# A fused linear attention and ELU feed-forward: the second group's attention by rows and DMA transposes

## The chip, the core and the metric

The kernel runs on one core of one Trainium2 chip. The metric is the device time of one execution in microseconds (us). A core has five engines, each with an instruction queue of its own that it works through in order: TensorE (PE in the profile, with PEld for its weight loads), VectorE (DVE), ScalarE (ACT), GpSimd (POOL) and SyncE (SP, which here only issues DMAs). Matmul results are written to PSUM, everything else lives in SBUF. Sixteen DMA engines move data between memory and SBUF, and can transpose on the way.

## The reference

Eight batches, eight heads, 576 positions, head size 64; then a feed-forward layer with 512 inputs, 2048 hidden units and 512 outputs for all 4608 tokens. Cut to its core:

```python
kv  = np.einsum('bhsd,bhse->bhde', k, v)          # one 64x64 matrix per batch and head
out = np.einsum('bhsd,bhde->bhse', q, kv)
rms = np.sqrt(np.mean(out * out, axis=-1, keepdims=True) + 1e-06)
x   = (out / rms * g_norm)                        # then laid out as 4608 x 512
h   = x @ w_in
g   = np.where(h > 0.0, h, np.exp(np.minimum(h, 0.0)) - 1.0)
result = g @ w_out
```

All matmuls take bf16 inputs and sum in fp32.

## The kernel before, in words

The tokens are worked in nine groups (0 to 8, called `T`) of 512. A position inside a batch is split into 9 slots of 64 rows, so a group holds eight slots, of one or two batches (`slot_of`, line 75).

For each group three things are done: the attention, which gives `xT` (the normed attention output, features on the partitions); the first product, eight tiles `mm1(T, i)` of eight 128x512 matmuls each (line 378), whose results `h_ps` go through the ELU into `gT`; and the second product into `o_ps` (line 399), 64 matmuls, called here in eight halves of eight matmuls: `mm2_half(T, n)` is row block `n // 2` and, by `n % 2`, the first or last half of the 16 hidden blocks. The finished row block is copied by ACT (line 415) and stored by SP.

The ELU of a tile has an ACT part, the exponential of `h_ps` (line 350), and a DVE part, `rest()`: `min(e, 1) - 1` (line 358) and then a maximum with `h_ps` (line 362). DVE thus reads `h_ps` last, and the PSUM buffer of the tile is free when the rest is done. With `relu=True` ACT also writes `relu(h_ps)` (line 354), the buffer is free after that, and DVE adds two SBUF tiles instead.

Attention comes in two forms.

- By columns (`Turned`, line 216): q is transposed by matmuls against an identity (`q_t_mm`, line 174) and copied into `qT`; the product with `kv` gives the output already turned (`y_mm`, line 189); ACT squares it; a matmul with a block of ones sums the squares (`mean_mm`, line 199); ACT takes the inverse root (lines 208, 209); DVE scales into `xT` (line 212).
- By rows (`attention`, line 258): q is loaded raw in fp32 (`fetch_ahead`), cast and reordered by POOL (`cast_q`, line 103) and turned by two DMA transposes issued by SP (`turn_q`, line 331). Per half of the group (`h` 0 and 1) the pieces are: `se`, 16 or 24 small matmuls (line 250) into the one buffer named `at` and ACT's square of it; `sum`, DVE's sums (line 283); `inv`, two small ACT steps (lines 291, 292); `mul`, DVE's scaling out of `at` (line 299) and two DMA transposes on SP into `xT` (line 306); `gain`, DVE's factor `g` on `xT` (line 312). The piece `kv` is the k-v product, also into `at`.

`after_turn` puts a tiny POOL copy (the gate, line 339) that waits for the turned q; the next loads stand behind it on POOL.

The order is written out by hand: the framework keeps each engine's instructions in program order and adds the waits. Before the change, group 0 and 1 have attention by columns, and group 2 too: its pieces (`late_kv`, `late_q`, `late_y`, `late_norm`, lines 697 to 717) stand between the tiles of group 1's first product and then between four halves of group 1's second product (lines 728 to 741). From group 3 on attention is by rows, inside `window` (line 747): tiles of the first product of group `T`, pieces of attention of `T + 1` and halves of the second product of `T - 1` alternate.

The kernel's PSUM pools hold eight buffers of 128x512 fp32. The tags A and B are a pair of them each, m two single ones, x two single ones in use until `start_psum.close()`, after which the same space is the `at` buffer, of which there is one. A matmul into a buffer waits until the last reader of its former content is done.

Apart from the first few, all loads are issued by POOL in the order of lines 484 to 508, each waiting for the load eight before it.

Of the kernel before, what the change touches and what calls it, by code (L numbers as in the profile page):

```python
# [16 lines left out]
def kernel(  # L17
# [14 lines left out]
    P = 128  # L32
# [48 lines left out]
    def fetch(name, b, u=None):  # L81

        if (name, b) not in bf:
            bf[name, b] = qkvp.tile([P, 4, RK, D], BF16, name=f"{name}_bf", tag=name)
        ms = slice(0, 4) if u is None else slice(u, 4, 2)
        load(bf[name, b][:, ms], name, b, ms)
# [5 lines left out]
    def fetch_ahead(b):  # L92
        raw[b] = stage.tile([P, 4, RK, D], FP32, name="st_q", tag="q")
        load(raw[b], "q", b)
        for name in "kv":
            fetch(name, b)
# [32 lines left out]
    def single(tag, name):  # L129
        pool = ps_x if tag == "x" else ps_m2  # L130
        return pool.tile([P, 512], FP32, name=name, tag=tag)

    def pair(tag, name):
        if tag in "xm":
            return [single(tag, name) for _ in range(2)]
        return ps_m1.tile([P, 2, 512], FP32, name=name, tag=tag)

    def as_bf16(ps):
        return ps.bitcast(BF16)
# [3 lines left out]
    def qT_tile(b):  # L143
        qT[b] = attp.tile([P, 2, 2, RK, 64], BF16, name="qT", tag="qT", bufs=3)
        return qT[b]

    def x_tile(T):
        xT[T] = attp.tile([P, KC, G], BF16, name="xT", tag="xT")
        return xT[T]

    def kv_mm(b, kv_ps, u, ls=range(2)):
        for j in range(RK):
            for s in range(2):
                rows = slice(s * 64, s * 64 + 64)
                for l in ls:
                    nc.tensor.matmul(  # L156
                        kv_ps[s][l * 64 : l * 64 + 64, u * 64 : u * 64 + 64],
                        lhsT=bf["k", b][rows, 2 * l + u, j, :],
                        rhs=bf["v", b][rows, 2 * l + u, j, :],
                        start=(j == 0),  # L160
                        stop=(j == RK - 1),
                    )

    def kv_out(b, kv_ps, u, engs):
        for s in range(2):
            copy_on(engs[s], kv_sb[:, b, u, s], kv_ps[s][:, u * 64 : u * 64 + 64])
# [4 lines left out]
    def q_t_mm(b, u, js, dst):  # L171
        for n, j in enumerate(js):
            for l in range(2):
                nc.tensor.transpose(  # L174
                    dst[l * 64 : l * 64 + 64, n * P : n * P + P], bf["q", b][:, 2 * l + u, j, :], ident
                )

    def q_t_out(b, u, eng, src, js):
        copy_on(eng, qT[b][:, :, u, js, :], src.rearrange("p (j s r) -> p s j r", s=2, r=64))
# [148 lines left out]
    def turn_q(b):  # L328
        qt = qT_tile(b)
        for s in range(2):  # L330
            nc.sync.dma_start_transpose(
                out=qt[:, s].rearrange("p u j r -> p (u j) r"),
                in_=bf["q", b][s * 64 : s * 64 + 64].rearrange("p u j l d -> p (u j l d)"),
            )

    def after_turn(b):

        gate = const.tile([1, 2, 16], BF16, name="gate")
        nc.gpsimd.tensor_copy(out=gate, in_=qT[b][0:1, :, 1, RK - 1, 0:16])  # L339
# [46 lines left out]
    def mm1(T, i, tag, relu=False):  # L386
        if i == 0:
            g_tile(T)
        ps = pair(tag, "h_ps")
        mm1_part(T, i, ps, range(KC))  # L390
        return elu(T, i, ps, relu)

    o_ps, o_sb = {}, {}
# [53 lines left out]
    def mm2_half(T, i):  # L447
        mm2(T, i // 2, 8 * (i % 2), 8 * (i % 2) + 8)
# [52 lines left out]
    for name in "kvq":  # L501
        fetch(name, 1, 1)
    load_w_out(3)
    for u in range(2):
        for name in "qkv":
            fetch(name, 2, u)
    fetch_ahead(3)
    cast_q(3)

# [11 lines left out]
    def turned_q(b, u, tag):  # L521

        ps = as_bf16(single(tag, "qt_ps"))
        q_t_mm(b, u, range(8), ps)
        return ps
# [42 lines left out]
                stop=(c == KC - 1),  # L568
            )

    qT_tile(0)
    x_tile(0)
    g_tile(0)
    g_ps = pair("A", "g_ps")
# [72 lines left out]
    def mm2_all(f0, f1, js=(2, 3, 0, 1)):  # L647
        for f in range(f0, f1):
            for j in js:
                mm2(0, j, f, f + 1)  # L650
# [4 lines left out]
            o_ps[0, j0 + t] = ps[:, t, :]  # L655

    x_tile(1)
    qT_tile(1)
    for u in range(2):
        n = Turned(1, u)  # L660
        if u == 0:
            mm2_all(0, 4, (2, 3))
        kv_ps = [single("x", "kv_ps") for _ in range(2)]
        kv_mm(1, kv_ps, u)
        kv_out(1, kv_ps, u, (A, A))
        if u == 0:
            mm2_all(0, 4, (0, 1))
        main = turned_q(1, u, "m")
        q_t_out(1, u, V, main, slice(0, 8))
        ends = as_bf16(single("m", "qt_ps"))  # L670
        for t in range(2):
            q_t_mm(t, u, (8,), ends[:, t * P : t * P + P])
        for t in range(2):
            q_t_out(t, u, V, ends[:, t * P : t * P + P], slice(8, 9))
        mm2_all(*((4, 6), (10, 11))[u])
        n.product([single("x", "y_ps") for _ in range(2)])
        for l in range(2):
            n.square(l)
        mm2_all(*((6, 7), (11, 12))[u])
        for l in range(2):  # L680
            n.sums(l, single("m", "mean"))
            n.inv(l)
            n.scale(l)
        mm2_all(*((7, 10), (12, 15))[u])
    for js in ((2, 3), (0, 1)):
        for j in js:
            mm2(0, j, 15, 16, out=False)
        for j in js:
            mm2_out(0, j)

    qT_tile(2)
    x_tile(2)
    n2 = [Turned(2, 0), Turned(2, 1)]

    def late_kv(u, tag):
        kv_ps = pair(tag, "kv_ps")
        kv_mm(2, kv_ps, u)
        kv_out(2, kv_ps, u, (A, A))  # L700

    def late_q(u, tag):
        main = turned_q(2, u, tag)
        end = as_bf16(single(tag, "qt_ps"))
        q_t_mm(2, u, (8,), end[:, 0:P])
        q_t_out(2, u, A, main, slice(0, 8))
        q_t_out(2, u, V, end[:, 0:P], slice(8, 9))

    def late_y(u):
        n2[u].product(pair("xm"[u], "y_ps"))  # L710
        for l in range(2):
            n2[u].square(l)

    def late_norm(u, l):
        n2[u].sums(l, single("mx"[u], "mean"))
        n2[u].inv(l)
        n2[u].scale(l)

    pieces = {
        1: lambda: late_kv(0, "x"),  # L720
        2: lambda: late_kv(1, "m"),
        3: lambda: late_q(0, "x"),
        4: lambda: (late_q(1, "m"), turn_q(3), after_turn(3), fetch_ahead(4)),
        5: lambda: late_y(0),
        6: lambda: late_norm(0, 0),
        7: lambda: late_norm(0, 1),
    }
    for i, tag in enumerate("mBABABAB"):
        rest = mm1(1, i, tag)
        rest()  # L730
        if i in pieces:
            pieces[i]()
    for j, tag in enumerate("AB"):
        o_ps[1, j] = pair(tag, "o_ps")[:, 0, :]
    mm2_half(1, 0)
    late_y(1)
    mm2_half(1, 2)
    late_norm(1, 0)
    mm2_half(1, 1)
    late_norm(1, 1)  # L740
    mm2_half(1, 3)
    start_psum.close()
    ps_at = ctx.enter_context(tc.tile_pool(name="ps_at", bufs=1, space=bass.MemoryType.PSUM))

    def window(T, at, early, late, second):
        for i in range(8):
            rest = mm1(T, i, "AB"[i % 2])
            for name in early.get(i, ()):  # L750
                at[name]()
            if i in second:
                second[i]()
            rest()
            for name in late.get(i, ()):
                at[name]()

    for T in range(2, NT):
        at, early, late = {}, {}, {}
        if T + 1 < NT:  # L760
            at = attention(T + 1)
            if T + 2 < B:
                cast_q(T + 2)

                def ahead(b=T + 2):
                    turn_q(b)
                    if b + 1 < B:
                        after_turn(b)
                        fetch_ahead(b + 1)
                at["ahead"] = ahead  # L770
            else:
                at["ahead"] = lambda: None
            early = {2: ("sum0", "inv0"), 4: ("sum1", "inv1"), 5: ("gain0",), 7: ("gain1",)}
            late = {0: ("kv",), 1: ("se0",), 2: ("mul0",), 3: ("se1",), 4: ("mul1", "ahead")}
        if T == 2:
            early = {2: ("sum0", "inv0"), 5: ("sum1", "inv1"), 6: ("gain0",), 7: ("gain1",)}
            late = {0: ("kv",), 1: ("se0",), 2: ("mul0",), 4: ("se1",), 5: ("mul1", "ahead")}
        halves = {0: 4, 2: 5, 4: 6, 6: 7} if T == 2 else {0: 1, 1: 3, 2: 4, 3: 5, 4: 6, 5: 7}
        second = {i: (lambda n=n: mm2_half(T - 1, n)) for i, n in halves.items()}
        window(T, at, early, late, second)  # L780
        mm2_half(T, 0)
        mm2_half(T, 2)
# [33 lines left out]
```

## Time and profile before

| | |
|---|---|
| median of 9 runs | 292.03 us (291.77 to 292.22) |
| the profiled execution | 292.11 us |
| its span, first to last instruction | 290.3 us |
| mean granted TensorE clock | 0.998 |
| PE busy | 279.9 us, 2109 matmuls seen |
| DVE busy | 165.8 us |
| ACT busy | 141.8 us |
| first matmul of the first product of group 1 | 48.69 us |
| of group 2 | 75.43 us |
| of group 3 | 101.97 us |

The last three are taken from the trace in order of time and the chain of waits. A line of the profile names the source line, engine, operation, output and input tiles, shape and count; behind the bar stand the group's busy time, the mean of one in ns, and the idle time of the engine ahead of it with what ended that. In a line in order of time, the bracket holds the same. Some matmul records are missing from a trace.

### The profile page before, as it was taken

To read this page: it belongs to the slowest core of one execution; us is meant where nothing else is said; L and a number is where in the kernel's file an instruction comes from. 1 tells how busy PE (TensorE), PEld (TensorE's weight loads), DVE (VectorE), ACT (ScalarE), POOL (GpSimd) and SP (SyncE) were. 2 spreads that over 40 slices of the span, in tenths; PEclk is the share of its full clock that TensorE was granted. 3 is DMA by queue.
4 is the path that set the end of the run, shared out by engine and by line. 5 is a ranking of instruction groups with operands and counts; after the bars stand their busy time and mean duration, and the time that the engine had idled before them with its cause. 6 is when DMAs were issued, how large, how long until landed. Compare 5 with 4: busy or idle time off the path is not lost.

```text
span 290.3 us, 5146 instructions
## 1 busy us (share of the span) xinstructions
PE 279.9 (96%) x2109; PEld 130.2 (45%) x2145; DVE 165.8 (57%) x223; ACT 141.8 (49%) x207; POOL 47.1 (16%) x85
## 2 busy tenths in 40 slices
PE   8899999999999999999999999999999999999994
PEld 3444444443444444444444444444444444444443
DVE  2349632776368747863776377636774776344600
ACT  3578358587555435543554255525552555343320
POOL 7643341404200022203400330000000000000000
PEclk9999999999999999999999999999999999999999
DMA  7999999997901299958965894452340215020222
GB/s 212 183 204 206 207 206 236 305 193 207 194 2 36 46 170 240 172 99 231 217 81 92 220 238 79 86 107 72 38 102 6 75 36 108 0 75 0 72 75 73
DMA packets 46332, 37.77 MB, mean 130 GB/s; under 512 B 26468, under 2 KB 40036, under 8 KB 46308
## 3 DMA queue, kind: packets, MB, share of 16 engines
q0 software_dynamic: 15312, 20.71, 36.8%
q1 hardware_dynamic: 30592, 16.19, 27.2%
q10 hardware_dynamic: 404, 0.53, 0.5%
q8 instruction: 17, 0.28, 0.4%
q14 instruction: 7, 0.06, 0.1%
HBM read 36.70 MB, written 9.44 MB: 159 GB/s over the span
## 4 chain that ended last, share of the span: by engine, by line
PE 88%; DVE 4%; ACT 3%; DMA 2%; issue 1%; SPq 0%; DVEq 0%
PE o_ps L399 40%; PE h_ps L378 39%; DMA first_v<-in_v_dram 2%; PE h_ps L563 2%; DVE gT L362 2%; PE at L250 2%; PE at L156 1%; ACT elu_e L350 1%; PE kv_ps L156 1%; PE qt_ps L174 1%; DVE xT L212 1%; PE mean L199 1%; PE y_ps L189 1%; DVE elu_e L358 1%; ACT rT L209 1%
## 5 line engine op out<-in xcount | busy, mean ns | idle before, releaser
L399 PE MATMUL o_ps<-w_out_sb,gT 128*128 128x512 bf16 x548 | 129.2, 379 | 1.3 <-DVE gT L362 0.6
L378 PE MATMUL h_ps<-xT,w_in_sb 128*128 128x512 bf16 x530 | 126.9, 379 | 1.9 <-DVE gT L362 0.6
L350 ACT ACTIVATE elu_e<-h_ps 128x1024 bf16<-128x1024 f32 (+1 forms) x77 | 73.8, 974 | 91.6 <-PE h_ps L378 79.7
L362 DVE TENSOR_TENSOR gT<-elu_e,h_ps 128x1024 bf16<-128x1024 bf16 (+1 forms) x74 | 84.6, 1148 | 7.2
L399 PEld LDWEIGHTS <-gT 128*128 128x128 bf16 x560 | 54.3, 98 | 66.5 <-issue 2.0
L378 PEld LDWEIGHTS <-w_in_sb 128*128 128x128 bf16 x552 | 52.4, 98 | 62.4 <-issue 1.7
L358 DVE TENSOR_SCALAR elu_e<-elu_e 128x1024 bf16<-128x1024 bf16 x72 | 31.6, 440 | 69.4 <-ACT elu_e L350 69.2
L415 ACT COPY o_sb<-o_ps 128x512 f32<-128x512 f32 x32 | 18.4, 587 | 18.9 <-PE o_ps L399 18.1
L103 POOL CAST q_bf<-st_q 128x384 bf16<-128x384 f32 x30 | 14.4, 523 | 28.0 <-DMA st_q<-in_q_dram 24.3
L212 DVE SCALAR_TENSOR_TENSOR xT<-y_ps,g_col,rT 128x512 bf16<-128x512 f32 (+1 forms) x14 | 9.1, 671 | 15.4 <-ACT rT L209 13.4
L283 DVE TENSOR_REDUCE ss<-sq 128x16 f32<-128x1024 bf16 x12 | 14.6, 1219 | 4.6 <-ACT sq L277 4.5
L299 DVE TENSOR_TENSOR xs<-at,ss 128x1024 bf16<-128x1024 f32 x12 | 14.6, 1216 | 0.0
L277 ACT ACTIVATE sq<-at 128x1024 bf16<-128x1024 f32 x12 | 12.3, 1028 | 1.0 <-PE at L250 1.0
L339 POOL COPY gate<-qT 1x32 bf16<-1x32 bf16 x4 | 0.8, 200 | 72.0 <-DMA qT<-q_bf 72.0
L156 PEld LDWEIGHTS <-k_bf 64*64 64x64 bf16 x576 | 6.5, 107 | 6.4 <-issue 6.4
L90 POOL DMA_DIRECT2D k_bf<-in_k_dram x12 | 8.4, 700 | 5.4 <-DMA w_out_sb<-in_moe_w_out_dram 2.1
L90 POOL DMA_DIRECT2D v_bf<-in_v_dram x12 | 8.3, 693 | 5.7 <-DMA w_in_sb<-in_moe_w_in_dram 2.1
L208 ACT ACTIVATE rT<-mean,eps_col 128x512 f32<-128x512 f32 (+1 forms) x9 | 6.6, 730 | 2.4 <-PE mean L199 2.2
L229 ACT ACTIVATE sq<-y_ps 128x512 bf16<-128x512 f32 x8 | 4.3, 596 | 6.5 <-PE y_ps L189 6.5
L112 DVE COPY o_sb<-o_ps 128x256 f32<-128x256 f32 x1 | 0.4, 423 | 11.5 <-DMA out_dram<-o_sb 11.5
L312 DVE TENSOR_SCALAR xT<-xT,g_col 128x1024 bf16<-128x1024 bf16 x12 | 5.7, 478 | 1.7 <-DMA xT<-xs 1.7
L519 PE MATMUL kv_ps<-zeros 128*128 128x512 bf16 x13 | 5.3, 574 | 1.2 <-DVE one L512 1.2
(56 smaller groups left out, 110.5 us busy)
## 6 DMA issues: line engine op xcount, KB each, us to landing
out_dram<-o_sb SPq DMA_DIRECT2D x24, 256.0 KB, 3.9
st_q<-in_q_dram POOLq DMA_DIRECT2D x5, 1152.0 KB, 7.6
k_bf<-in_k_dram POOLq DMA_DIRECT2D x5, 576.0 KB, 10.9
v_bf<-in_v_dram POOLq DMA_DIRECT2D x5, 576.0 KB, 13.6
out_dram<-o_sb SPq DMA_DIRECT2D x19, 128.0 KB, 2.6
w_out_sb<-in_moe_w_out_dram POOLq DMA_DIRECT2D x4, 512.0 KB, 15.0
q_bf<-in_q_dram POOLq DMA_DIRECT2D x5, 288.0 KB, 13.4
k_bf<-in_k_dram POOLq DMA_DIRECT2D x4, 288.0 KB, 14.2
```

The source lines that it names most:

```text
L90: eng.dma_start(out=dst.rearrange("p m j d -> p m (j d)"), in_=in_[:, ms, :])
L103: nc.gpsimd.tensor_copy(out=bf["q", b][:, u, js], in_=raw[b][:, u::2, js, :].rearrange("p l j d -> p j l d"),)
L156: nc.tensor.matmul(kv_ps[s][l * 64 : l * 64 + 64, u * 64 : u * 64 + 64], lhsT=bf["k", b][rows, 2 * l + u, j, :], rhs=bf["v", b][rows, 2 * ...
L277: nc.scalar.activation(sq, st["se", h], AF.Square)
L283: nc.vector.reduce_sum(out=ss, in_=st.pop(("sq", h)).rearrange("p l (m e) -> p (l m) e", e=D), axis=AX.X,)
L299: nc.vector.tensor_tensor(out=st["xs"][:, 2 * h : 2 * h + 2, :].rearrange("p i (l m e) -> p l i m e", l=2, e=D), in0=se_ps.rearrange("p l ...
L350: nc.scalar.activation(e[:, lo:hi, :], h, AF.Exp)
L358: nc.vector.tensor_scalar(out=e, in0=e, scalar1=1.0, scalar2=1.0, op0=ALU.min, op1=ALU.subtract)
L362: nc.vector.tensor_tensor(out=gT[T][:, 2 * i + lo : 2 * i + hi, :], in0=e[:, lo:hi, :], in1=h, op=ALU.add if relu else ALU.max,)
L378: nc.tensor.matmul((ps[a] if isinstance(ps, list) else ps[:, a, :])[:, cols], lhsT=w_in_sb[:, c, f * P : f * P + P], rhs=xT[T][:, c, cols] ...
L399: nc.tensor.matmul(o_ps[T, j], lhsT=gT[T][:, f, j * P : j * P + P], rhs=w_out_sb[:, f, :], start=(f == 0), stop=(f == FC - 1),)
L415: nc.scalar.copy(o_sb[T, half][:, j % 2, :], o_ps[T, j])
```

## The change

Group 2's attention goes from columns to rows. Its q, k and v are loaded whole (q raw), cast by POOL, and q is turned by DMA ahead of batch 3's loads. Its kv product stands behind tile 2 of group 1's first product, its first row product behind tile 3, its second behind tile 6. Tiles 4, 5 and 7 of group 1 take the relu form of the ELU, the tiles' PSUM tags become m, B, A, m, B, A, m, B, and DVE's sums and scalings of group 2 stand ahead of the rests of tiles 4 to 7. Five halves of group 1's second product follow (row blocks 0 and 1 whole, and the first half of block 2), then the two gains; the last three halves stand in group 2's window, where there were four. The tags of every window's tiles swap from A, B to B, A. The transposes of group 2 and the turn of batch 3 on SP now stand after group 1's tiles. In group 0's second product, which stands between the steps of group 1's attention, the stretch behind the first half's scaling grows from hidden blocks 7 to 9 to blocks 7 to 10, and the one behind the second half's shrinks by one block.

```diff
@@ loads
-    for u in range(2):
-        for name in "qkv":
-            fetch(name, 2, u)
+    for b in range(2):
+        qT_tile(b)
+    fetch_ahead(2)
+    cast_q(2)
+    turn_q(2)
+    after_turn(2)
     fetch_ahead(3)
     cast_q(3)
@@ group 0's second product, group 1's attention
-        mm2_all(*((4, 6), (10, 11))[u])
+        mm2_all(*((4, 6), (11, 12))[u])
...
-        mm2_all(*((6, 7), (11, 12))[u])
+        mm2_all(*((6, 7), (12, 13))[u])
...
-        mm2_all(*((7, 10), (12, 15))[u])
+        mm2_all(*((7, 11), (13, 15))[u])
@@ group 1's first product and group 2's attention
-    pieces = {
-        1: lambda: late_kv(0, "x"),
-        2: lambda: late_kv(1, "m"),
-        3: lambda: late_q(0, "x"),
-        4: lambda: (late_q(1, "m"), turn_q(3), after_turn(3), fetch_ahead(4)),
-        5: lambda: late_y(0),
-        6: lambda: late_norm(0, 0),
-        7: lambda: late_norm(0, 1),
-    }
-    for i, tag in enumerate("mBABABAB"):
-        rest = mm1(1, i, tag)
-        rest()
-        if i in pieces:
-            pieces[i]()
-    for j, tag in enumerate("AB"):
-        o_ps[1, j] = pair(tag, "o_ps")[:, 0, :]
-    mm2_half(1, 0)
-    late_y(1)
-    mm2_half(1, 2)
-    late_norm(1, 0)
-    mm2_half(1, 1)
-    late_norm(1, 1)
-    mm2_half(1, 3)
     start_psum.close()
     ps_at = ctx.enter_context(tc.tile_pool(name="ps_at", bufs=1, space=bass.MemoryType.PSUM))
+    at = attention(2)
+    rest = {}
+    for i, tag in enumerate("mBAmBAmB"):
+        rest[i] = mm1(1, i, tag, i in (4, 5, 7))
+        if i == 2:
+            at["kv"]()
+        if i == 3:
+            at["se0"]()
+        if i == 5:
+            at["sum0"]()
+            at["inv0"]()
+            at["mul0"]()
+            rest[4]()
+        if i == 6:
+            at["se1"]()
+            rest[5]()
+        if i < 4:
+            rest[i]()
+    at["sum1"]()
+    at["inv1"]()
+    rest[6]()
+    at["mul1"]()
+    rest[7]()
+    turn_q(3)
+    after_turn(3)
+    fetch_ahead(4)
+    ps = pair("A", "o_ps")
+    for j in range(2):
+        o_ps[1, j] = ps[:, j, :]
+    for f0, f1 in ((0, 8), (8, 12)):
+        for j in range(2):
+            mm2(1, j, f0, f1)
+    mm2_half(1, 4)
+    for j in range(2):
+        mm2(1, j, 12, 16, out=False)
+    for j in range(2):
+        mm2_out(1, j)
+    at["gain0"]()
+    at["gain1"]()
@@ windows
-            rest = mm1(T, i, "AB"[i % 2])
+            rest = mm1(T, i, "BA"[i % 2])
...
-        halves = {0: 4, 2: 5, 4: 6, 6: 7} if T == 2 else {0: 1, 1: 3, 2: 4, 3: 5, 4: 6, 5: 7}
+        halves = {1: 5, 3: 6, 5: 7} if T == 2 else {0: 1, 1: 3, 2: 4, 3: 5, 4: 6, 5: 7}
```

More of the change, by code (lines that the diff above doesn't have):

```diff
@@ L569, in early @@
             )
-    qT_tile(0)
     x_tile(0)
@@ L657 @@
     x_tile(1)
-    qT_tile(1)
     for u in range(2):
@@ L689 @@
             mm2_out(0, j)
[L693 to L717, printed above, removed]
-    pieces = {
-        1: lambda: late_kv(0, "x"),
-        2: lambda: late_kv(1, "m"),
-        3: lambda: late_q(0, "x"),
-        4: lambda: (late_q(1, "m"), turn_q(3), after_turn(3), fetch_ahead(4)),
-        5: lambda: late_y(0),
-        6: lambda: late_norm(0, 0),
-        7: lambda: late_norm(0, 1),
-    }
-    for i, tag in enumerate("mBABABAB"):
-        rest = mm1(1, i, tag)
-        rest()
-        if i in pieces:
-            pieces[i]()
```

## The prediction

> **What bounds the kernel now.** I read the page's busy shares first, then its slices, then stretches of time around the change, then the queues of the loads, then instruction groups. All times below are microseconds (us) from the start of the profiled execution.
>
> The page, busy time and slices:
> ```profile
> PE 279.9 (96%) x2109; PEld 130.2 (45%) x2145; DVE 165.8 (57%) x223; ACT 141.8 (49%) x207; POOL 47.1 (16%) x85
> ...
> DVE  2349632776368747863776377636774776344600
> ...
> PEclk9999999999999999999999999999999999999999
> DMA  7999999997901299958965894452340215020222
> ```
> TensorE (PE) is busy nearly always at full clock, so a gain must come from fewer matmuls or from PE's few idle stretches; and the DMA engines are full until slice 9 (65 us). Stretches of time (length, then busy time per engine):
> ```profile
> 50.00:60.00 10.00, 9.55 (x141) 4.83 (x141) 6.75 (x10) 6.33 (x13) 2.94 (x6) 1.00 1.11 303
> 60.00:70.00 10.00, 8.91 (x58) 3.72 (x54) 7.90 (x12) 8.45 (x12) 2.45 (x4) 1.00 0.84 164
> ...
> 80.00:90.00 10.00, 9.89 (x70) 4.55 (x69) 7.09 (x9) 5.88 (x9) 0.00 (x0) 1.00 0.02 3
> ```
> In group 1 (first product from 48.69, group 2's from 75.43) PE loses 0.45 and 1.09; later stretches lose about 0.1. That is the place. GpSimd (POOL) and the SyncE queue (SPq) in order of time (start, length, what), with the wait before each in brackets:
> ```profile
> 37.53 0.70 POOL L90 DMA_DIRECT2D k_bf<-in_k_dram  x1 [0.72 <-DMA k_bf<-in_k_dram]
> 38.93 0.71 POOL L90 DMA_DIRECT2D v_bf<-in_v_dram  x1 [0.70 <-DMA v_bf<-in_v_dram]
> 40.36 0.75 POOL L90 DMA_DIRECT2D st_q<-in_q_dram  x1 [0.72 <-DMA q_bf<-in_q_dram]
> 43.23 0.74 POOL L90 DMA_DIRECT2D k_bf<-in_k_dram  x1 [2.12 <-DMA w_out_sb<-in_moe_w_out_dram]
> ...
> 54.47 2.94 POOL L103 CAST q_bf<-st_q 128x384 bf16<-128x384 f32 x6 [9.03 <-DMA st_q<-in_q_dram]
> ...
> 57.44 5.88 SPq L331 DMA_TRANSPOSE qT<-q_bf  x2
> ...
> 65.40 0.20 POOL L339 COPY gate<-qT 1x32 bf16<-1x32 bf16 x1 [7.99 <-DMA qT<-q_bf]
> ...
> 99.94 3.53 SPq L331 DMA_TRANSPOSE qT<-q_bf  x2
> ...
> 106.43 0.20 POOL L339 COPY gate<-qT 1x32 bf16<-1x32 bf16 x1 [31.84 <-DMA qT<-q_bf]
> ```
> Each POOL load waits for the one eight before it, so these releases tell landings: half loads land every 1.4, and the last w_out quarter landed at 43.2. Batch 3's q came raw at 54.4, was cast until 57.4, turned by SyncE (SP) from 57.44, and the gate tells that the turn had landed at 65.35: 7.9 for the turn with k and v of batch 3 still loading, and 6.5 (99.94 to 106.43) without. Groups by shape:
> ```profile
> L174 PE MATMUL qt_ps<-ident,q_bf 128*64 128x128 bf16 x108 | 4.2, 224 | 0.1
> L350 ACT ACTIVATE elu_e<-h_ps 128x1024 bf16<-128x1024 f32 x67 | 68.6, 1024 | 90.5 <-PE h_ps L378 79.7 <-remote 9.5 <-issue 1.4
> L354 ACT ACTIVATE elu_h<-h_ps 128x1024 bf16<-128x1024 f32 x3 | 3.1, 1036 | 0.0
> L299 DVE TENSOR_TENSOR xs<-at,ss 128x1024 bf16<-128x1024 f32 x12 | 14.6, 1216 | 0.0
> L283 DVE TENSOR_REDUCE ss<-sq 128x16 f32<-128x1024 bf16 x12 | 14.6, 1219 | 4.6 <-ACT sq L277 4.5
> ```
> These are the unit prices of what goes and comes.
>
> **The change part by part**, as the place of the first matmul of group 3, at 101.97 before. Behind it both programs do the same work.
>
> *PE's work.* Removed: 36 transposes (two pieces of 0.69 = 1.38), 16 y products (2 x 0.34), 4 mean products (0.29 each by the chain of waits, 1.16): 3.2. Added: two pieces of 16 row products, 0.34 each: 0.7. Net 2.5 less. One half (8 matmuls, 1.73) moves from group 2's window to ahead of it, which alone costs nothing while PE is the bound.
>
> *Group 0's second product.* One f-step (4 matmuls, 0.86) moves from the second norm to the first. That covers PE's wait on the last scaling (0.36 idle at 41.4, "DVE xT"). The second attention half then runs about 0.35 later and 0.86 less stands behind it, so group 1's first product starts near 48.4, not 48.69. Its last input chunk is then scaled at 48.8, and matmuls on the other three chunks cover that. Gain 0.3; bounds 0 and 0.6.
>
> *Loads.* Six half loads of batch 2 become raw q, k, v, directly behind w_out. Raw q: 43.2 + 2.8 (54.4 less 43.2 less six times 1.4) = 46.0. POOL casts 2.94, to 49.0. SP turns; the group 0 stores queue behind it on SP and nobody waits for those. With k and v loading at the same stage as for batch 3, 7.9: landed at 56.9. Bounds: 6.5 gives 55.5, and 2 later if the loads share worse. Batch 3's loads wait for the gate and come from 57 on, 14 us later than now; its turn follows group 2's transposes on SP from about 73.3 and lands near 79.8, needed at 81.2: hidden by 1.4. Batch 4's, now at 66, go to 80; its turn is at 98 or so: hidden by over 5.
>
> *The page on the turn.* The Trainium skill, "DMA: Bandwidth & Descriptors", section "Latency and other measured facts", gives 261 GB/s for a transpose with a non-contiguous middle dimension; an estimate from it for a 576 KB batch of q is 2.3. The rows above say 6.5 and 7.9, and the sum goes by them; by the page the turn would be in time and the forecast 0.8 lower.
>
> *Group 1's first product.* Eight tiles of 1.73, in order. Tiles 0 to 3 with the kv product (0.78) end at 48.4 + 6.9 + 0.8 = 56.1. The row product then waits for the turn: 0.8, to 56.9. VectorE's (DVE) ELU rests of tiles 0 to 2 are done by 56.4, so no PSUM buffer holds PE there. Tiles 4, 5, 6 end at 62.5. Next comes the second row product, which needs the one `at` buffer, free only after mul0. On ScalarE (ACT) inv0 stands behind exp and relu of tiles 4 and 5: from tile 4's end (59.05) four steps at 0.92 apart (the issue distance of such steps at 26.5 to 30.1) end at 62.9, inv0 adds 0.4, mul0 on DVE 1.22: 64.5. PE idles 2.0. Bounds: 1.5 if inv0 slips in sooner, 2.6 if every ACT step takes its full 1.03. Queued behind mul0 on DVE are the rests of tiles 4 and 5, behind the waiting row product on PE tile 7. Tile 7 ends at 66.65.
>
> *Five halves, then group 2.* 5 x 1.73 = 8.63 from 66.65: 75.3. DVE meanwhile: rests 4 and 5 (1.14 each), sum1 1.22, rest 6 1.8, mul1 1.22: from 64.5 to 70.7, every rest done before its half asks. From the end of mul1 the two transposes and the gain take 3.75 (97.32 to 101.07 before) and 0.48: 75.0. Batch 3's k and v may still be loading then; transposes landed in 2.4 to 5.7, so 0 to 3.3 more. I take 0.5, as only the tail of v is left: group 2 starts at 75.5.
>
> *Group 2's window.* 13 x 1.73 + kv 0.75 + row products 0.81 = 24.0. The window before measured 26.54 for 25.74 of work; without its 0.35 wait on scaling the same overhead is 0.45. With one half less, DVE (8 rests of 1.66 and two times 1.22 + 1.22 + 0.48, 19.1) has less slack: I take 0.4 for a wait on the last gain, bounds 0 and 1. Group 3 starts at 75.5 + 24.9 = 100.4.
>
> *Sum.* 101.97 - 100.4 = 1.55 less. The profiled execution took 292.11 (span 290.3 and 1.8 around it), 0.08 above the median of 292.03, so 290.5.
>
> *A rule against it.* The forecast gap of 2.0 has no like behind the start before, and no slice shows a lower clock. The Trainium skill, "TensorE: Matmul & The Clock Gate", section "Why this matters for your kernels", warns against PE idle gaps of more than about 3 us, which drop the clock to half; if the gap did that for a stretch of 4 us, an estimate from the page is 2 more.
>
> **The rivals.**
> - *No wait for the turn (faster still).* The raw load may land before 46.0, as stores of group 0 ran beside it before (49.6 to 56) and now come behind. Then 0.8 goes and the last gains come without a wait (0.5): 289.2 to 289.6. Against it: the queue's even 1.4 pace.
> - *The turn lands late (slower).* Place: the first row product. Each us of delay beyond 56.9 costs one, as everything hangs behind it in PE's order. It decides from 58.4; slower by over 0.2% from 59.0. At 60: 293.6. For it: DMA is full there (share 1.0 to 1.36 at 59 to 65). Against: batch 3 had the same neighbours and took 7.9.
> - *Waits eat it all (same).* The transposes of group 2 land at 5.7 each time and the window waits 1 on the gain: +1.3 to 1.6, 291.8 to 292.2.
> - *It does nothing:* excluded, since 48 rows of PE's instruction order (matmuls and weight loads) are gone and PE carries the path.
>
> **How the numbers follow.** 0.2% is 0.58, about what a measurement can tell: faster is below 291.45, slower above 292.61. Likeliest 0.50 (290.5; its own range 289.7 to 291.4), no wait 0.20, late turn 0.18, eaten 0.12. Faster 0.70, same 0.12, slower 0.18. The range 289.0 to 292.9 leaves out most of the late turn and a little below.
>
> **What would show it.** PE idle about 0.8 before the first row product, ended by the DMA of qT; about 2.0 before the second, ended by DVE xs L299; group 2's first product at 75 to 76; group 3's near 100.4; POOL's gate near 57. Wrong if the gate stands after 59, if the idle before the second row product exceeds 3, or if the clock drops behind it.

## The result and the profile after

The changed kernel takes 290.34 us in the median (289.73 to 291.44, 11 runs) against 292.06 for the kernel before (33 runs): a ratio of 0.9943, 95% interval 0.9932 to 0.9955, or 1.7 us faster. The forecast was 290.5.

The profiled execution (290.42, span 288.6) in the places that the prediction named, by the view in order of time:

| start of | before | forecast | after |
|---|---|---|---|
| group 1's first product | 48.69 | 48.4 | 48.02 |
| group 2's first row product | - | 56.9 | 55.94 |
| its second row product | - | 64.5 | 63.73 |
| group 2's first product | 75.43 | 75.5 | 75.19 |
| group 3's first product | 101.80 | 100.4 | 100.46 |

The 101.97 for group 3 before, from which the prediction starts, is of the chain of waits, which counts a matmul from the end of the one ahead of it; in order of time it is 101.80. The two executions are 0.1 apart already ahead of every edit: the first attention product of group 1 (L189) starts at 36.33 before and at 36.23 after.

The page of the changed kernel, busy time and three of its slice rows:

```profile
PE 276.5 (96%) x2085; PEld 128.8 (45%) x2121; DVE 166.8 (58%) x225; ACT 138.0 (48%) x201; POOL 49.1 (17%) x89
...
PE   7899999979999999999999999999999999999994
...
PEclk9999999999999999999999999999999999999999
DMA  7999999899799649968935992542140235030222
```

PE is busy 3.4 us less and the span is only 1.7 shorter. Most of the difference is new waiting, above all in slice 8 (counted from 0: 57.7 to 64.9 us). The waits of TensorE, longest in total first (us in total, times, longest):

```profile
PE at L250 <- DVE xs L299: 2.1, 1, 2.1
...
PE h_ps L378 <- DVE xT L312: 1.0, 2, 0.6
```

The same kernel in order of time, the lines around these waits:

```profile
54.75 0.21 POOL L339 COPY gate<-qT 1x32 bf16<-1x32 bf16 x1 [6.54 <-DMA qT<-q_bf]
...
60.95 1.04 ACT L354 ACTIVATE elu_h<-h_ps 128x1024 bf16<-128x1024 f32 x1
61.85 0.33 ACT L291 ACTIVATE ss<-ss,eps_col 128x16 f32<-128x16 f32 x1
...
62.46 1.22 DVE L299 TENSOR_TENSOR xs<-at,ss 128x1024 bf16<-128x1024 f32 x1 [2.83 <-ACT ss L292]
63.52 4.06 POOL L103 CAST q_bf<-st_q 128x384 bf16<-128x384 f32 x6 [5.98 <-DMA st_q<-in_q_dram]
63.60 0.70 DVE L358 TENSOR_SCALAR elu_e<-elu_e 128x1024 bf16<-128x1024 bf16 x1
...
63.73 0.41 PE L250 MATMUL at<-kv_sb,qT 64*128 64x64 bf16 x16 [2.10 <-DVE xs L299]
...
74.60 0.49 DVE L312 TENSOR_SCALAR xT<-xT,g_col 128x1024 bf16<-128x1024 bf16 x1 [2.40 <-DMA xT<-xs]
...
75.19 1.89 PE L378 MATMUL h_ps<-xT,w_in_sb 128*128 128x512 bf16 x7 [0.58 <-DVE xT L312]
```

The turn of q had landed by 54.75 and nothing waits for it. Then the chain is as forecast: ACT's relu of tile 5 stands in front of the small inverse-root step (L291), that in front of DVE's scaling (L299), and that in front of the second row product, for which TensorE idles 2.10. DVE's steps beside POOL's cast are slow (0.70 for what takes 0.43 elsewhere), and the last gain comes 0.58 after TensorE could have gone on.

One more thing is in the runs. Each shows the mean granted TensorE clock over its span. Beside the eleven of the median a twelfth is on record (289.88), and the twelve lie in two groups, called heaps below:

```text
clock 0.998 or 0.999: 289.73 289.88 289.93 290.02 290.06 290.27 290.34 290.42   (mean 290.08)
clock 0.993 or 0.994: 290.82 290.84 291.42 291.44                               (mean 291.13)
```

The kernel before showed 0.996 to 1.000 in the 48 runs of it that were taken along with the experiments. So the median of 290.34 is that of a mixture; the profiled execution is one in which the clock held.

### The profile page after: what moved, and what is told of

Its sections match the earlier page's. It is cut to its first block, busy times and chain, and to the rows that moved or that the text cites. A ratio compares the mean times of both kernels' runs of the same rounds, so it can differ in the third digit from the quotient of the medians.

```text
span 288.6 us, 5107 instructions
## 1 busy us (share of the span) xinstructions
PE 276.5 (96%) x2085; PEld 128.8 (45%) x2121; DVE 166.8 (58%) x225; ACT 138.0 (48%) x201; POOL 49.1 (17%) x89
## 4 chain that ended last, share of the span: by engine, by line
PE 85%; DVE 6%; DMA 4%; issue 2%; ACT 1%; SPq 1%; DVEq 0%
PE h_ps L378 38%; PE o_ps L399 37%; DVE gT L362 2%; DMA first_v<-in_v_dram 2%; PE h_ps L566 2%; DMA xT<-xs 2%; PE at L250 2%; PE at L156 2%; PE o_ps L436 1%; DVE elu_e L358 1%; PE kv_ps L156 1%; DVE xs L299 1%; PE mean L199 1%; DVE ss L283 1%; ACT elu_e L350 1%
## 5 line engine op out<-in xcount | busy, mean ns | idle before, releaser
L362 DVE TENSOR_TENSOR gT<-elu_e,h_ps 128x1024 bf16<-128x1024 bf16 (+1 forms) x73 | 81.0, 1118 | 7.2 <-PE h_ps L378 0.5
L103 POOL CAST q_bf<-st_q 128x384 bf16<-128x384 f32 x36 | 18.2, 550 | 34.7 <-DMA st_q<-in_q_dram 34.7
L283 DVE TENSOR_REDUCE ss<-sq 128x16 f32<-128x1024 bf16 x14 | 17.0, 1218 | 4.8 <-ACT sq L277 4.8
L299 DVE TENSOR_TENSOR xs<-at,ss 128x1024 bf16<-128x1024 f32 x14 | 17.0, 1218 | 2.8 <-ACT ss L292 2.8
L277 ACT ACTIVATE sq<-at 128x1024 bf16<-128x1024 f32 x14 | 14.4, 1027 | 0.8 <-PE at L250 0.8
L212 DVE SCALAR_TENSOR_TENSOR xT<-y_ps,g_col,rT 128x512 bf16<-128x512 f32 (+1 forms) x10 | 6.2, 641 | 11.0 <-ACT rT L209 9.0
L312 DVE TENSOR_SCALAR xT<-xT,g_col 128x1024 bf16<-128x1024 bf16 x14 | 6.7, 480 | 4.7 <-DMA xT<-xs 4.7
L250 PE MATMUL at<-kv_sb,qT 64*128 64x64 bf16 (+1 forms) x248 | 6.1, 193 | 2.1 <-DVE xs L299 2.1
L250 PEld LDWEIGHTS <-qT 64*128 64x128 bf16 (+1 forms) x248 | 4.4, 97 | 8.2 <-issue 8.0
L112 DVE COPY qT<-qt_ps 128x1024 bf16<-128x1024 bf16 (+1 forms) x8 | 3.3, 453 | 5.0 <-PE qt_ps L174 5.0
```

What stands on the lines that cost most here:

```text
L103: nc.gpsimd.tensor_copy(out=bf["q", b][:, u, js], in_=raw[b][:, u::2, js, :].rearrange("p l j d -> p j l d"),)
L250: nc.tensor.matmul(se_ps[lo:hi, l, (4 * i + m) * 64 : (4 * i + m) * 64 + 64], lhsT=qT[b][l * 64 : l * 64 + 64, s, u, j : j + n, :], rhs=kv ...
L283: nc.vector.reduce_sum(out=ss, in_=st.pop(("sq", h)).rearrange("p l (m e) -> p (l m) e", e=D), axis=AX.X,)
L299: nc.vector.tensor_tensor(out=st["xs"][:, 2 * h : 2 * h + 2, :].rearrange("p i (l m e) -> p l i m e", l=2, e=D), in0=se_ps.rearrange("p l ...
L362: nc.vector.tensor_tensor(out=gT[T][:, 2 * i + lo : 2 * i + hi, :], in0=e[:, lo:hi, :], in1=h, op=ALU.add if relu else ALU.max,)
```

## The experiments

**Stand-ins.** All experiments have plain copies in place of the DMA transposes: same bytes, same queue, same waits. What is told apart is thus the order of work and its waits, on a kernel that is not quite the changed one; so the kernels before and after were run with stand-ins too. Line numbers are higher by two or so; `e` is the length of a run in elements.

```diff
-            nc.sync.dma_start_transpose(
-                out=qt[:, s].rearrange("p u j r -> p (u j) r"),
-                in_=bf["q", b][s * 64 : s * 64 + 64].rearrange("p u j l d -> p (u j l d)"),
-            )
+            nc.sync.dma_start(
+                out=qt[:, s].rearrange("p u j r -> p (u j r)").rearrange("p (x e) -> p x e", e=e),
+                in_=bf["q", b].rearrange("p u j l d -> p (u j l d)").rearrange("p (x t e) -> p t x e", t=2, e=e)[:, s],
+            )
...
-                    nc.sync.dma_start_transpose(
-                        out=xT[T][:, :, i * P : i * P + P], in_=st["xs"][:, i, :]
-                    )
+                    nc.sync.dma_start(
+                        out=xT[T][:, :, i * P : i * P + P],
+                        in_=st["xs"][:, i, :].rearrange("p (c e) -> p c e", e=P),
+                    )
```

> A measurement by itself, for the size of a stand-in. The changed kernel with every DMA transpose replaced by a plain copy of the same bytes on the same queue and behind the same waits; the transposition is left out, so q and the attention output reach the matmuls unturned. The copies of q go in runs of 64 elements for batches 2 and 5, 32 for 3 and 6, 128 for 4 and 7. The transposes took 6.5 us from SyncE's start to the gate, and 2.5 us to land one of an attention output. Expected: runs of 64 nearest to 6.5 (4 to 7), of 32 longer, of 128 shorter; the copies of the attention output 2.0 to 2.5. If the copies land within 1 us of the transposes, the time is 290.3 within 0.6.

From SyncE's start to the gate, the copies took 6.9 us (batch 2, 48.30 to 55.19) and 6.0 (batch 5) in runs of 64, 8.7 in runs of 32, 4.9 in runs of 128. Runs of 64 were kept. The time, 291.12, is near the slower heap of the changed kernel, and the stretches of time of this run show why (length, busy per engine, then the granted clock as the third number from the end):

```profile
62.00:64.00 2.00, 0.00 (x0) 0.00 (x0) 1.25 (x2) 1.66 (x5) 0.00 (x0) 1.00 1.13 214
64.00:66.00 2.00, 1.79 (x20) 0.95 (x21) 1.93 (x4) 1.02 (x1) 0.75 (x2) 0.67 1.20 205
66.00:68.00 2.00, 2.00 (x6) 0.68 (x5) 1.90 (x4) 0.26 (x1) 2.00 (x4) 0.50 1.18 198
```

TensorE does nothing from 62 to 64, the wait for the second row product, and directly behind it the clock is at half.

> The kernel before with stand-ins: every DMA transpose replaced by a plain copy of the same bytes on the same queue behind the same waits, in runs of 64 elements for q; the transposition is left out. Expected 292.0 within 0.3, if the stand-ins do for the transposes.

> The changed kernel with the same stand-ins (transposition left out). Expected 290.3 within 0.6, the runs lying in two heaps as those of the changed kernel do: near 290.0 at a granted clock of 0.998 or more, near 291.1 at 0.994 or less.

With stand-ins the kernel before takes 291.71 (ratio to the kernel before 0.9990, 0.9981 to 0.9998). The changed one shows both heaps, further apart: three runs at 289.04 to 289.27 with the clock held, five at 290.88 to 291.33 at 0.994, median 290.88 (0.9943, 0.9919 to 0.9966). A dropped clock costs 1.9 here and 1.0 in the changed kernel itself. That the changed kernel hides part of it, because its group 2 starts late for the last gain anyway, is argued, not shown. The stand-ins do not do for the transposes in one place: where the clock holds the time is 289.1, and not the 290.0 expected, and TensorE no longer waits for the last gain (group 2's first product starts at 74.27, against 75.19 with transposes).

**The idle filled.**

```diff
         if i == 6:
+            idle(9, pair("B", "fill")[:, 0, :])
             at["se1"]()
```

> The changed kernel with stand-ins (transposition left out); nine matmuls of zeros into the free buffer of tile 7 stand ahead of the second row product, so TensorE works through 1.9 of its 2.1 us of waiting and nothing else moves. Theory (the idle makes the granted clock drop in some runs, and that costs them 1.1): every run has a clock of 0.998 or more and the heap near 291.1 is gone, 290.1. Rival (the drop has another cause): some runs still show 0.994 and 291.

Measured 289.14 (288.96 to 289.60, ratio 0.9905, 0.9892 to 0.9918), every clock 0.997 or more. Nothing starts earlier; the second row product stands at 63.55, as at 63.56 with stand-ins alone. So the clock drop comes from the idle, and 289.14, which is also the mean of the three runs above in which the clock held, is the mark for the experiments that follow.

**A part of the idle filled**, with `idle(2, ...)` in the same place.

> The changed kernel with stand-ins (transposition left out), with two matmuls of zeros ahead of the second row product instead of nine, so that about 1.7 us of idle is left. Theory (a clock drop needs an idle of about 2 us at the right moment, and idles of 1.3 and 1.5 did none): fewer runs at 0.994 than in the changed kernel with stand-ins (5 of 8), perhaps none; 289.1 where the clock holds. Rival (any idle over 1.5 does it): about as many as without filling.

Measured 289.24, all four runs at 0.999 or 1.000, with an idle of 1.7 left. So 1.7 did not drop the clock in four runs, where 2.1 did in five of eight; if it dropped the clock as often, four such runs in a row would come up about once in fifty. (The 1.5 in the expectation is two idles, 0.97 and 0.48; the longest single one seen by then without a drop was 1.26.)

**The first scaling ahead of tile 5's ScalarE steps.**

```diff
-        if i == 5:
+        if i == 4:
             at["sum0"]()
             at["inv0"]()
             at["mul0"]()
+        if i == 5:
             rest[4]()
```

> The changed kernel with stand-ins (transposition left out); group 2's first sums, inverse root and scaling are recorded behind tile 4 instead of tile 5, so that on ScalarE the two small steps come ahead of tile 5's exp and relu. Theory (the idle of 2.1 us before the second row product is two ScalarE steps in front of the inverse root, and it is on the path): the idle falls to about 0.2, group 2's first product starts near 72.7 instead of 75.2, the clock never drops, the time is 288.0. Rival (VectorE's work from tile 4 to the last gain binds whatever the order): group 2 starts at 74.5 or later, 289.7 or more.

The waits of TensorE in this run that answer to those of the changed kernel:

```profile
PE at L250 <- DVE xs L299: 0.3, 1, 0.3
...
PE h_ps L380 <- DVE xT L313: 0.2, 1, 0.2
```

Measured 288.07 (0.9864, 0.9849 to 0.9879), clocks 0.998 to 1.000: 1.1 below the filled idle and 2.8 below the median with stand-ins alone. The idle fell from 2.1 to 0.3. From the first row product to group 2's first product it took 16.7 (56.28 to 72.95) against 18.5 (55.77 to 74.27), 1.8 less. The theory holds; group 2 began at 72.95, against 74.27 with stand-ins alone. This is the fastest version found; it was run with stand-ins only, so what it gives with transposes, where the last gain lands later, is not shown.

**Tile 7 ahead of the second row product.**

```diff
         if i == 6:
-            at["se1"]()
             rest[5]()
+        if i == 7:
+            at["se1"]()
```

> The changed kernel with stand-ins (transposition left out); the second row product stands behind tile 7 instead of ahead of it, so TensorE has tile 7 to do while the scaling of the first half ends. To be held against the run with the filled idle, 289.1, in which the clock does not drop either. Theory (the path runs from the first scaling over ScalarE and VectorE to the last gain, and TensorE only shows it): an idle of 1.5 to 1.9 us moves to the place ahead of group 2's first product, which still starts at 74.2 to 74.8; 289.1 within 0.5, or more if that idle drops the clock. Rival (TensorE's idle is itself the cost): 1.7 less, 287.4.

```profile
PE o_ps L401 <- DVE gT L364: 1.5, 2, 1.0
PE h_ps L380 <- DVE xT L313: 1.3, 1, 1.3
```

Measured 290.63 (0.9953, 0.9941 to 0.9965): 1.5 slower than the filled idle, where the theory said the same and the rival 1.7 faster. TensorE had its work, and waited 2.8 later, for the rests and the last gain. Both had left something out: the square of the second row product now stood behind tile 7's exp and relu on ScalarE (67.07 to 68.10, and the second scaling at 70.99 instead of 69.14), so the edit made the chain itself longer. What the idle alone is worth is therefore read from the run with the filled idle, the last gain and group 2's first product:

```profile
73.61 0.49 DVE L313 TENSOR_SCALAR xT<-xT,g_col 128x1024 bf16<-128x1024 bf16 x1 [1.15 <-DMA xT<-xs]
...
74.27 1.89 PE L380 MATMUL h_ps<-xT,w_in_sb 128*128 128x512 bf16 x8
```

The gain ends at 74.10, 0.17 ahead of the product that needs it. With the chain to the gain unchanged, TensorE could have started no more than 0.2 earlier, whatever was done with its idle. So the idle is not by itself the loss; the chain through ScalarE and VectorE, which holds the second row product and the last gain alike, is.

**Four halves instead of five.**

```diff
-    mm2_half(1, 4)
...
-        halves = {1: 5, 3: 6, 5: 7} if T == 2 else ...
+        halves = {0: 4, 2: 5, 4: 6, 6: 7} if T == 2 else ...
```

> The run with the filled idle (stand-ins, transposition left out, 289.1), but with four halves of group 1's second product ahead of group 2 instead of five, and four in its window as before. Theory (the fifth half covers the landing of group 2's transposes and its gain): TensorE waits 1.3 to 1.5 ahead of group 2's first product, which starts near 74.1, the window is longer by 1.7 less 0.4 of waits that go, 290.1, and more where the clock drops. Rival (a half costs the same on either side): 289.1.

```profile
74.45 1.89 PE L380 MATMUL h_ps<-xT,w_in_sb 128*128 128x512 bf16 x8 [1.26 <-DVE xT L313]
```

Measured 290.23 (0.9940, 0.9927 to 0.9952), 1.1 more than with five. The wait of 1.26 for the gain is there. The fifth half covers the landing of what stands for group 2's transposes.

**The turn late.**

```diff
 def fetch_ahead(b):
     raw[b] = stage.tile([P, 4, RK, D], FP32, name="st_q", tag="q")
+    if b == 2:
+        for name in "kv":
+            fetch(name, b)
     load(raw[b], "q", b)
-    for name in "kv":
-        fetch(name, b)
+    if b != 2:
+        for name in "kv":
+            fetch(name, b)
```

> The run with the filled idle (stand-ins, transposition left out, 289.1), but batch 2's k and v are loaded ahead of its raw q. The raw q then lands 5.6 later, near 51.0, its turn near 59.7 instead of 55.2. Theory (each us that the turn lands behind 55.8 costs one): the first row product waits 3.8 to 4.0, 293.0, and up to 295 if that idle drops the clock. Rival (the waits further on take it up): 290.5 or less.

The wait of TensorE, then stretches of this run:

```profile
PE at L254 <- DMA qT<-q_bf: 4.5, 2, 2.6
```

```profile
58.00:60.00 2.00, 0.20 (x2) 0.10 (x2) 0.32 (x1) 0.00 (x0) 0.00 (x0) 0.76 0.77 111
60.00:62.00 2.00, 1.21 (x9) 0.58 (x10) 0.00 (x0) 0.83 (x1) 0.78 (x2) 0.50 0.97 239
62.00:64.00 2.00, 2.00 (x6) 0.65 (x5) 1.22 (x1) 0.20 (x1) 1.69 (x3) 0.50 0.93 257
64.00:66.00 2.00, 2.00 (x6) 0.76 (x5) 0.00 (x0) 1.30 (x2) 0.00 (x0) 0.53 0.99 298
```

Measured 296.67 (1.0147, 1.0123 to 1.0171), 7.5 above the filled idle. The turn had landed at 60.9 and the row product waited 4.5. Every run shows a dropped clock (0.988 to 0.993), and the rest above 4.5, some 3, goes with it: the two runs at 0.992 and 0.993 took 294.95 and 295.23, the four at 0.988 296.30 to 297.16, and in the trace the 24 matmuls of tiles 4 to 6 took 7.71 (from 61.06) instead of 5.35. Nothing further on took the delay up. So had the turn come late, the kernel would have ended slower, as that rival of the prediction said, and by more than the one us per us that was put on it.

**The moved blocks of group 0's second product alone**, on the kernel before:

```diff
-        mm2_all(*((4, 6), (10, 11))[u])
+        mm2_all(*((4, 6), (11, 12))[u])
...
-        mm2_all(*((6, 7), (11, 12))[u])
+        mm2_all(*((6, 7), (12, 13))[u])
...
-        mm2_all(*((7, 10), (12, 15))[u])
+        mm2_all(*((7, 11), (13, 15))[u])
```

> The kernel before with stand-ins (transposition left out, 291.7), with only the moved blocks of group 0's second product. Theory (it covers the wait of 0.36 on the last scaling of group 1's first half): group 1's first product starts 0.3 to 0.5 earlier, 291.3. Rival (the wait turns up elsewhere): 291.7.

The wait, in the kernel before:

```profile
41.39 0.47 PE L156 MATMUL kv_ps<-v_bf,k_bf 64*64 64x64 bf16 x34 [0.36 <-DVE xT L212]
```

Measured 291.50 against 291.71 (0.9976, 0.9968 to 0.9985, against 0.9990, 0.9981 to 0.9998). The wait on the scaling is gone from the list of waits. The traces say more than the times, if both are counted from the first attention product of group 1 (L189), ahead of the edit, at 36.19 without it and 36.56 with it: from there group 1's first product comes 0.57 earlier (48.55 and 48.35), and group 3's 0.47 (101.70 and 101.60, by the chain of waits). So the theory holds in its place. In time the gain is 0.2 by the medians and 0.4 by the ratios, and the intervals overlap: its size there is not settled.

**The cast late**, on the filled idle:

```diff
     fetch_ahead(3)
-    cast_q(3)
...
     rest[6]()
+    held = const.tile([1, 2, 16], BF16, name="held")
+    nc.gpsimd.tensor_copy(out=held, in_=gT[1][0:1, 12:14, 0:16])
+    cast_q(3)
     at["mul1"]()
```

> The run with the filled idle (stand-ins, transposition left out, 289.1), but GpSimd's cast of batch 3's q waits for the rest of tile 6. Theory (the cast slows the steps of VectorE beside it, 0.42 and 0.69 to 0.72 and 0.87): the rests of tiles 4 and 5 return to 0.42 and 0.69, the second scaling starts 0.6 to 0.9 earlier, and the time hardly moves, 288.9 to 289.2, since with the stand-ins the last gain is not what group 2's first product waits for. Rival (the slow steps come from something else, such as ScalarE writing the same tiles): they stay at 0.72 and 0.87.

The run in order of time: tile 4's first step, then the cast and tile 7's first step beside it:

```profile
63.73 0.42 DVE L360 TENSOR_SCALAR elu_e<-elu_e 128x1024 bf16<-128x1024 bf16 x1
...
69.01 2.77 POOL L103 CAST q_bf<-st_q 128x384 bf16<-128x384 f32 x6
69.84 2.21 DVE L360 TENSOR_SCALAR elu_e<-elu_e 128x1024 bf16<-128x1024 bf16 x1
```

The rests of tiles 4 and 5 are back at 0.42 and 0.69, and the step that now lies beside the cast takes 2.21, to just behind the end of the cast at 71.78. The cast is the cause. The second scaling follows the second row product after 4.84 instead of 5.59 (63.87 to 68.71, 63.55 to 69.14), 0.75 sooner, as expected, and the time, 289.28 (289.13 to 289.66), did not move.

**No relu form.**

```diff
-        rest[i] = mm1(1, i, tag, i in (4, 5, 7))
+        rest[i] = mm1(1, i, tag)
```

> The changed kernel with stand-ins (transposition left out), without the relu form in tiles 4, 5 and 7. Theory (the inverse root waits for four ScalarE steps, so two fewer free the buffer of the second row product 1.8 earlier, while the rest of tile 4, now the last reader of tile 7's buffer, comes late): the idle before the second row product falls to 0.5 or less, tile 7 waits 1.2 to 1.6 for DVE gT instead, 288.6 to 289.4, the clock holds. Rival (the relu form carries the change, as it frees buffers): 290.5 or more.

```profile
PE h_ps L380 <- DVE gT L364: 1.6, 2, 1.2
...
PE at L250 <- DVE xs L299: 1.1, 1, 1.1
```

Measured 290.13 (289.45 to 291.52; 0.9940, 0.9918 to 0.9962). The wait before the row product is 1.1 instead of 2.1, but not the 0.5 expected, and tile 7 waits 1.25 for DVE, as expected. The two idles lie 0.4 apart, and two of six runs show 0.994, against the expectation; the four others lie at 289.45 to 290.48, above the 289.04 to 289.27 with the relu form and the clock held. Neither the theory's 289.4 nor the rival's 290.5 was met. So the relu form carries neither the gain nor the wait alone: it trades one wait for the other, and is worth some tenths.

## Why the prediction was right, step by step

- *PE's work:* 2.5 net was forecast; TensorE's busy time fell by 3.4. The groups in question fell by 2.9 in all (transposes 4.2 to 2.8, y products 3.3 to 2.5, mean products 4.5 to 3.0, row products up from 5.3 to 6.1), where the busy times of groups overlap and count more than the engine's own. Right in kind and near in size.
- *Group 0's second product:* 0.3 was forecast, bounds 0 and 0.6. Group 1's first product came 0.67 earlier, 0.1 of it there ahead of the edit; the part alone gave 0.57. The mechanism was right and the gain near its upper bound.
- *Loads and the turn:* this step failed. It put the landing at 56.9, from 46.0 for the raw q and 7.9 for the turn. The cast began at 45.46 and the turn took 6.5 (48.24 to 54.75), the lower bound. The wait of 0.8 was not there; what was given the chance of 0.20 is what happened at this place, though that rival's time, 289.2 to 289.6, was not. The estimate of 2.3 for a turn from the Trainium skill, "DMA: Bandwidth & Descriptors", section "Latency and other measured facts", was further off than either row. The turn of batch 3 came as forecast: from 73.39, landed by 79.91, needed at 81.28.
- *The second row product:* right, mechanism and size: 2.0 forecast, 2.10 measured, and the early scaling took it away.
- *The last gain:* mis-sized. From the end of the first scaling to the end of the second the sum had 6.2, and its own terms add up to 6.5; it took 7.1 (63.68 to 70.75). The rests of tiles 4 and 5 took 3.1 for the 2.3 that was put on them, as POOL's cast of batch 3 lay beside their four DVE steps; the prediction had counted the cast on its own queue only. The 0.5 allowed for a late landing was not needed (3.85 from the end of the second scaling to the gain, where 3.75 and 0.5 were added up). TensorE waited 0.58, where the sum had 0.2. That the cast slows such steps is shown; that it delayed the start of group 2 is read from this one trace, as with the stand-ins alone TensorE does not wait there.
- *Group 2's window:* 24.9 forecast, 25.27 measured; the wait on the last gain in it is 0.40, as taken. Of the rest the trace names a wait of 0.17 at 89.34, for the ELU.
- *The clock:* the sum had nothing for it, and the prediction had named a drop behind this idle as a sign of being wrong. It came in 4 of 12 runs, at a cost of 1.0, where the prediction had estimated 2. The Trainium skill, "TensorE: Matmul & The Clock Gate", section "Why this matters for your kernels", warns from about 3 us on. Here an idle of 2.1 was enough. The rule was the right one to weigh, and its threshold too high for this place.
- *The sum* was right within 0.2 partly by luck. The first scaling ended 0.8 earlier than forecast, the steps to the second took 0.9 more, the landing 0.4 less, and the window 0.4 more: group 3 stands at 100.46 for 100.4. In order of time this is 1.34 less than before, where the sum had about 1.55; the 0.35 that is left of the 1.7 comes behind group 3, where the sum had nothing, and no run shows why. And the median is one of two heaps, at 290.08 and 291.13.

## What to carry to other kernels

A stall of TensorE is worth tracing to the chain behind it before it is filled: putting the next tile into it cost 1.5 us, as the chain grew longer by it, while moving two small ScalarE steps ahead of two large ones gave 1.1 us, and more where the clock had dropped. In this kernel an idle of about 2 us could cost half of its length to all of it again in clock. When a DMA is moved ahead of a product, look at its margin: here it landed 1.2 us ahead of need, and with stand-ins a load order by which it landed 5.6 us later cost 7.5. And two traces are best compared from a common point ahead of the edit: their starts differ by some tenths, as much as the parts to be told apart.

## What had not been expected of the hardware

- The mean granted clock fell to 0.994 or less behind an idle of 2.1 us in 4 of 12 runs of the changed kernel and 5 of 8 with stand-ins, and in 2 of 6 with two idles of 1.1 and 1.25 us that lay 0.4 apart; with 1.7 us left of the idle it fell in none of four. The three traces of runs with a dropped clock (the first with stand-ins, the turn late, no relu form) have it at 0.50 for some microseconds.
- A GpSimd cast from fp32 to bf16 slowed two kinds of VectorE steps beside it that work from SBUF to SBUF: `min(e, 1) - 1` went from 0.42 to 0.70, 0.72 and once 2.21, and the addition of two tiles from 0.69 to 0.87. The cast of six pieces went from 2.8 to 4.06 in the changed kernel, and stayed at 2.77 where the step took 2.21. VectorE's scaling out of PSUM (1.22, from 68.71 in the run with the cast late) and its sums (1.21, from 66.68 in the changed kernel) lay beside the same cast unchanged.
- Plain copies of q in runs of 128 bytes took as long as the DMA transposes of the same bytes (6.0 to 6.9 us against 6.5).
